# One-hots of both choices in one operation each, shared ports in the order model, and early stores on ScalarE

## The chip, the cores and the metric

The kernel runs on one core of a Trainium2 chip. A core has five engines that run beside each other, each through its own list of instructions in a fixed order: TensorE (PE, matrix products), VectorE (DVE), ScalarE (ACT), GpSimd (POOL) and SyncE (SP, which here only issues transfers). Data lies in DRAM and is brought by DMA queues into the on-chip memory SBUF; matrix products are written to PSUM. The metric is the time of one execution on the device in microseconds (us).

## The reference

Two stages. The first is a retention layer over q, k and v of shape [8 batches, 8 heads, 576 positions, 64]:

```
ret = (q k^T / 8) * D_h        D_h[i,j] = gamma_h^(i-j) for i >= j, else 0
x   = ret v                    -> 4608 tokens of 512 values
```

The second is a mixture of 8 experts. Each token gets noisy logits `x w_gate + log(1 + exp(x w_noise)) * noise`, and its two largest choose two experts, weighted by a softmax over the two. The output of a token is the sum over its two choices of

```
weight * ( relu(x w1[e]) w2[e] )      w1[e]: 512 x 1024,  w2[e]: 1024 x 512
```

## The kernel before

**Attention in units.** The 512 first positions are handled in 16 units, one for a batch and four of its heads. A unit loads q, k and v (`load`), scales and casts them to bf16 (`cast`: L436 for k, L442 for q, L449 for v), transposes them on PE (`tr`, L467), and then multiplies scores (`scores`, L492, masked on DVE at L500), carried states (`states`, L523) and outputs (`out_`, L555 and L565). The last 64 positions of a batch are the tails (`load_tail`, `tail`: L592, L601, L614, L619), two batches at a time.

**Routing per batch pair.** Two batches are a batch pair `bp`, 1152 tokens in 9 columns of 128. There are four, and each goes through `route` when its units and tails are done: logits, the two largest on DVE and POOL in some 25 small operations, the rank of each token within its expert by products with triangles of ones (L730, L732), and from the rank a place in the expert's list. The list itself, a table of the token number at each place, is built by a product of one-hots: `lof` and `hif` hold the low 7 bits of a place and the rest of it, for two choices x 9 columns. `olo` compares `lof` with 0..127 (L771), `oh` compares `hif` with 0..79 (L774), `oh` is multiplied by the token numbers `vals` (L777), and PE adds up the products of `olo` and `oh` over 18 pairs in a PSUM tile (`table`, L783), nine for each choice. DVE adds the result to the table so far and casts it to the list of rows `xi` (L790 to L796). Beside it, `route` puts the tokens with their payload (`pay`, L763 and L764, copied at L813) into rows that ACT stores to DRAM as `xd` (L816).

**Experts.** A tile is a group of rows of one expert. Rows are gathered from `xd` by `xi` with indirect transfers that POOL issues (`fetch`, L933), transposed on PE (L951), multiplied by w1 (`up`, L1005, or `wide`, L1031), passed through the relu (`relu`, L1014 on ACT or L1016 on DVE) and multiplied by w2 (`second`, L1080). `finish` scales the result by the gate. The first choice of a token goes to a DRAM buffer `yd` (evicted at L1114 or L1116, stored by SP at L1120), and the second one reads it back and adds it (L1095, L1124) and scatters the sum to the output (L1128). Tiles that the batch pairs 0 to 2 fill run early, for the experts 0 to 2, 15 blocks of 128 rows in all, between the units of the attention and behind the last route. The rest, which needs the last batch pair's list, runs afterwards as the wide phase, from 242 us of the profile on, where L1031 and L1080 alternate. Weights come through `weights`: those of experts 0 to 2 by casting transfers that POOL issues, the later ones by SP (L887 for w1, L890 for w2) into buffers of the class `big`, which the attention's inputs use before, and a cast by ACT or DVE.

**The order.** Nothing is issued where it stands in the code. `Plan.op` records an operation with its engine (or a choice of engines), an assumed cost, what it reads and writes, and a priority. `Plan.run` is a list scheduler: it keeps for each engine the time from which it is free, takes the ready operation that can start first, and appends it to the order. So each engine's fixed order comes from assumed costs, not measured times, and a change of one cost or engine can move operations everywhere. Transfers of SP and ACT share eight semaphores in turn; a transfer waits for the one that used its semaphore before. The lines of `run` that hold the model of time are

```
t = max(t0, free.get(e, 0.0))
...
free[e] = t + c
o.fin = t + c
```

In the profile `q` behind an engine's name is its issue of transfers, and PEld is PE's loading of the stationary operand.

Of the kernel before, what the change touches and what calls it, by code (L numbers as in the profile page):

```python
# [9 lines left out]
F16 = mybir.dt.float16  # L10
# [7 lines left out]
P = 128  # L18
# [32 lines left out]
class Op:  # L51
    __slots__ = ("i", "eng", "fn", "prio", "dma", "preds", "succ", "need", "allocs", "bufs", "fin", "on")


class Plan:
# [21 lines left out]
    def op(self, eng, cost, fn, r=(), w=(), prio=0.0, dma=0, after=()):  # L77
        o = Op()
        o.i, o.fn, o.prio, o.dma = len(self.ops), fn, prio, dma
        o.eng = eng if isinstance(eng, dict) else {eng: cost}  # L80
        o.succ, o.allocs, o.bufs = [], [], []
        preds = set(after)
        for items, wr in ((r, False), (w, True)):
            for it in items:
                b, sub = it if isinstance(it, tuple) else (it, None)
                for s2, o2, w2 in b.acc:
                    if (wr or w2) and (sub is None or s2 is None or s2 == sub):
                        preds.add(o2)
                if b not in o.bufs:
                    o.bufs.append(b)  # L90
        for items, wr in ((r, False), (w, True)):
            for it in items:
                b, sub = it if isinstance(it, tuple) else (it, None)
                if wr:
                    b.acc = [a for a in b.acc if a[1] is o or not (sub is None or a[0] == sub)]
                b.acc.append((sub, o, wr))
        preds.discard(o)
        for b in o.bufs:
            if b.cls is not None:
                if not b.ops:  # L100
                    o.allocs.append(b)
                    self.fifo.setdefault((b.cls, b.stream), []).append(b)
                b.ops.append(o)
                b.left += 1
        o.preds, o.need = preds, len(preds)
        for p in preds:
            p.succ.append(o)
        self.ops.append(o)
        return o

    def run(self):
        free, dma_free = {}, {}
# [33 lines left out]
        while ready:  # L146
            pick = None
            for o in ready:
# [38 lines left out]
            free[e] = t + c  # L187
            o.fin = t + c
# [39 lines left out]
class Kernel:  # L228
# [42 lines left out]
    def setup(self):  # L271
# [5 lines left out]
        def o(e, cost, b, fn, prio, r=()):  # L277
            pl.op(e, cost, lambda e: fn(), r=r, w=[b], prio=prio)
# [60 lines left out]
        vals = f("vals", [P, C9], F16)  # L339
        o("POOL", 0.2, vals, lambda: G.iota(vals.t, pattern=[[P, C9]], base=1, channel_multiplier=1, **n), 1)  # L340
# [79 lines left out]
    def cast(self, u):  # L420
# [16 lines left out]
        pl.op({"ACT": 1.06, "DVE": 0.7}, 0, k, r=[rk], w=[kn], prio=u)  # L437
# [5 lines left out]
        pl.op({"DVE": 1.23, "POOL": 1.91}, 0, q, r=[rq, tab], w=[qb], prio=u)  # L443
# [6 lines left out]
        for c in range(2):  # L450
            pl.op({"DVE": 0.69, "POOL": 1.06}, 0, lambda e, c=c: v(e, c), r=[(rv, c), tab], w=[(vn, c)], prio=u)
# [126 lines left out]
    def tail(self, bp, prio):  # L578
# [10 lines left out]
              else nc.vector.tensor_scalar_mul(qv(1), raw["k"].t, 0.125), r=[raw["k"]], w=[(qk, 1)], prio=prio)  # L589
        for j, n, o, b in ((8, "q", lambda: qv(0), (qk, 0)), (9, "v", vv, vt)):  # L590
# [3 lines left out]
                  r=[raw[n], tab], w=[b], prio=prio)  # L594
# [51 lines left out]
    def route(self, bp, prio):  # L646
# [7 lines left out]
        def o(e, cost, fn, r, w, prio=prio):  # L654
            return pl.op(e, cost, fn, r=r, w=w, prio=prio)
# [112 lines left out]
        iota, vals = self.fixed["iota"], self.fixed["vals"]  # L768
        olo, oh = f("olo", [P, 2, C, P], F16), f("oh", [P, 2, C, NH], F16)
        for j in range(2):  # L770
            o("DVE", 1.3, lambda e, j=j: V.tensor_tensor(  # L771
                olo.t[:, j], iota.t.unsqueeze(1).to_broadcast([P, C, P]), lof.t[:, j].unsqueeze(2).to_broadcast([P, C, P]),
                Alu.is_equal), [iota, lof], [(olo, j)])
            o("DVE", 0.9, lambda e, j=j: V.tensor_tensor(  # L774
                oh.t[:, j], iota.t[:, :NH].unsqueeze(1).to_broadcast([P, C, NH]),
                hif.t[:, j].unsqueeze(2).to_broadcast([P, C, NH]), Alu.is_equal), [iota, hif], [(oh, j)])
            o({"DVE": 0.9, "POOL": 1.4}, 0, lambda e, j=j: self.eng(e).tensor_tensor(  # L777
                oh.t[:, j], oh.t[:, j], vals.t.unsqueeze(2).to_broadcast([P, C, NH]), Alu.mult), [vals, (oh, j)], [(oh, j)])
        pT = self.psum("rt")

        def table(e, j):
            for c in range(C):
                nc.tensor.matmul(pT.t[:, :NH], lhsT=olo.t[:, j, c, :], rhs=oh.t[:, j, c, :],  # L783
                                 start=(j == 0 and c == 0), stop=(j == 1 and c == C - 1), skip_group_check=True)
        for j in range(2):
            o("PE", 0.6, lambda e, j=j: table(e, j), [(olo, j), (oh, j)], [pT])
# [313 lines left out]
    def finish(self, i, t, s, prio):  # L1100
# [8 lines left out]
        if k != "S":  # L1109
            y = pl.buf("half", "exp")  # L1110

            def ev(eng, y=y, po=po, g=g, n=n):
                if eng == "ACT":
                    nc.scalar.activation(y.t[:n], po.t[:n], Act.Copy, scale=g()[:n])  # L1114
                else:
# [4 lines left out]
            pl.op("SP", 0.07, lambda _, y=y, r0=r0, n=n: nc.sync.dma_start(out=self.yd[r0:r0 + n, :], in_=y.t[:n]),  # L1120
                  r=[y], w=[(key, j)], prio=prio, dma=0.7)
# [256 lines left out]
```

## Time and profile before

| what | value |
|---|---|
| time, median of 3 runs | 508.46 us (505.43 to 517.59) |
| time of the profiled execution | 505.94 us |
| span of the instructions in it | 504.4 us |
| PE busy | 419.5 us, 83% of the span |
| PE weight loads busy (beside PE) | 250.4 us, 50% |
| POOL busy | 303.2 us, 60% |
| ACT busy | 234.7 us, 47% |
| DVE busy | 199.8 us, 40% |
| mean granted TensorE clock | 0.927 of full speed |
| moved by DMA | 105.34 MB, mean 209 GB/s |

The span runs from the first to the last instruction; some 1.5 us of the execution lie around it. Times in the text are counted from the span's start. "L783" is line 783 of the kernel before. A wait is written as the instruction that waits, `<-`, and the instruction or transfer that ended last before it went on. Busy times are averages over parts of the kernel with different limits, so the text looks at windows of 20 us.

### The profile page before, as it was taken

What the parts mean: (1) busy time and instruction counts of PE and PEld (TensorE: products, weight loads), DVE (VectorE), ACT (ScalarE), POOL (GpSimd) and SP (SyncE); (2) the same over time, 40 slices, a digit from 0 to 9 for tenths busy, and PEclk for the clock granted to TensorE, in tenths of its full rate; (3) what the DMA queues carried; (4) which work ended last, traced back from release to release, by engine and by line L of the source; (5) the groups of instructions that cost most, each with busy time, mean ns of one, the idle gap of its engine ahead of it and who ended that gap; (6) DMA issues with size and microseconds to landing.
All of it is one profiled execution on the core that took longest, in us unless ns stands there. A gap on an engine that the chain in (4) does not pass through costs nothing. (4 is left out here: it accounts for less than half of the span.)

```text
span 504.4 us, 11045 instructions
## 1 busy us (share of the span) xinstructions
PE 419.5 (83%) x4253; PEld 250.4 (50%) x4288; DVE 199.8 (40%) x500; ACT 234.7 (47%) x397; POOL 303.2 (60%) x357
## 2 busy tenths in 40 slices
PE   1698948858678888729997999999899999899991
PEld 1476746646456667506544453453453453353450
DVE  3445697696348559500212333213214121121221
ACT  2476735556385556315654465545254242433330
POOL 8866599588769536773134544654756567357334
PEclk9995875888999989959998999999999999999997
DMA  7999979999698855434569797596589995525313
GB/s 188 304 248 305 241 218 302 226 287 209 171 187 141 206 94 179 144 98 128 216 205 339 239 329 244 161 313 239 167 265 371 254 214 180 153 103 189 109 52 138
DMA packets 102489, 105.34 MB, mean 209 GB/s; under 512 B 31870, under 2 KB 80511, under 8 KB 102434
## 3 DMA queue, kind: packets, MB, share of 16 engines
q1 hardware_dynamic: 82242, 62.85, 42.2%
q0 software_dynamic: 15264, 36.89, 28.1%
q10 hardware_dynamic: 4928, 4.87, 3.0%
q8 instruction: 34, 0.56, 0.5%
q14 instruction: 21, 0.17, 0.1%
HBM read 83.20 MB, written 26.63 MB: 218 GB/s over the span
## 5 line engine op out<-in xcount | busy, mean ns | idle before, releaser
L1080 PE MATMUL ps<-W,half 128*128 128x512 bf16 (+1 forms) x613 | 209.8, 391 | 22.0 <-issue 10.8
L1031 PE MATMUL ps<-big,W 128*128 128x512 bf16 (+4 forms) x632 | 187.2, 330 | 5.3 <-DVE half L1016 3.6
L1014 ACT ACTIVATE half<-ps 128x512 bf16<-128x512 f32 (+5 forms) x186 | 91.6, 505 | 155.1 <-PE ps L1031 85.4
L933 POOL DMA_INDIRECT xg<-xd,xi x80 | 83.1, 1039 | 80.3 <-ACT half L1114 29.7
L1080 PEld LDWEIGHTS <-half 128*128 128x128 bf16 (+1 forms) x640 | 63.1, 100 | 105.8 <-issue 38.3
L1031 PEld LDWEIGHTS <-W 128*128 128x128 bf16 x640 | 60.9, 98 | 56.5 <-issue 18.5
L1128 POOL DMA_INDIRECT out_dram<-half,xg x39 | 39.8, 1021 | 48.2 <-DVE half L1124 27.7
L1124 DVE SCALAR_TENSOR_TENSOR half<-ps,xg,half 128x512 f32<-128x512 f32 (+1 forms) x39 | 29.0, 749 | 88.8 <-PE ps L1080 52.2
L1095 POOL DMA_INDIRECT half<-yd,xg x39 | 39.6, 1016 | 11.9 <-issue 11.3
L262 ACT ACTIVATE half<-ps 128x1024 bf16<-128x1024 bf16 (+1 forms) x36 | 34.3, 988 | 17.0 <-DVE half L500 7.2
L500 DVE TENSOR_TENSOR half<-ps,mask 128x512 bf16<-128x512 f32 x64 | 40.0, 681 | 3.6 <-PE ps L492 2.6
L442 POOL TENSOR_TENSOR half<-big,tab 128x1024 bf16<-128x1024 f32 x15 | 29.5, 1967 | 12.6 <-DMA big<-in_q_dram 11.9
L467 PE MATMUL ps<-ident__69,half 128*128 128x128 bf16 x256 | 23.5, 259 | 11.7 <-ACT half L434 6.0
L449 POOL TENSOR_TENSOR half<-big,tab 128x512 bf16<-128x512 f32 x30 | 32.5, 1100 | 0.0
L1005 PE MATMUL ps<-half,W 128*128 128x256 bf16 (+1 forms) x288 | 30.5, 260 | 1.4 <-ACT tb L262 1.4
L523 PE MATMUL ps<-half,half 64*64 64x64 bf16 (+2 forms) x512 | 31.6, 235 | 0.2 <-issue 0.2
L1114 ACT ACTIVATE half<-ps,xg 128x512 f32<-128x512 f32 (+1 forms) x32 | 22.0, 688 | 16.8 <-PE ps L1080 9.8
L1005 PEld LDWEIGHTS <-W 128*128 128x128 bf16 x288 | 24.6, 100 | 6.0 <-issue 1.7
L262 ACT ACTIVATE xT<-ps 128x512 bf16<-128x512 f32 (+1 forms) x38 | 19.0, 554 | 15.6 <-PE ps L565 10.6
L467 PEld LDWEIGHTS <-half 128*128 128x128 bf16 x256 | 19.5, 118 | 13.2 <-ACT half L434 6.0
L523 PEld LDWEIGHTS <-half 128*64 128x64 bf16 (+1 forms) x512 | 19.5, 115 | 12.3 <-issue 4.1
L1124 DVE SCALAR_TENSOR_TENSOR half<-ps,gm,half 128x512 f32<-128x512 f32 x6 | 4.5, 751 | 52.8 <-ACT half L1114 35.0
(174 smaller groups left out, 455.7 us busy)
## 6 DMA issues: line engine op xcount, KB each, us to landing
big<-in_moe_w_dram SPq DMA_DIRECT2D x40, 512.0 KB
yd<-half SPq DMA_DIRECT2D x40, 256.0 KB
big<-in_k_dram SPq DMA_DIRECT2D x32, 256.0 KB
big<-in_q_dram SPq DMA_DIRECT2D x16, 512.0 KB
big<-in_v_dram SPq DMA_DIRECT2D x32, 256.0 KB
W<-in_moe_w_dram POOLq DMA_DIRECT2D x12, 512.0 KB
xd<-xg ACTq DMA_DIRECT2D x16, 264.0 KB
xg<-xd,xi POOLq DMA_INDIRECT x80
```

The costliest lines, as they stand in the source:

```text
L262: self.nc.scalar.activation(out, in_, Act.Copy)
L467: nc.tensor.transpose(v[:, hp, x, :], i[:, y, hp * P:(hp + 1) * P], ident.t)
L500: nc.vector.tensor_tensor(S.t.bitcast(BF16).rearrange("p (h c x) -> p h c x", h=2, c=2)[:, h], p[h].t.rearrange("p (c x) -> p c x", c=2), ...
L523: nc.tensor.matmul(o[h * HD:(h + 1) * HD, hp, n, :], lhsT=kv[0][:k, r, c, 2 * hp + h, :], rhs=m, start=(hp == 0 and c == 0 and k == P and ...
L933: pl.op("POOL", 1.3, lambda _, x=x, h=h, n=n: nc.gpsimd.indirect_dma_start(out=x.t[:n, :], out_offset=None, in_=self.xd[:rows, :], in_offs ...
L1005: nc.tensor.matmul(pv()[:, f2, :], lhsT=w.t[:, o:o + P], rhs=xv()[:, di, :n], start=(di == 0), stop=(di == KD - 1))
L1014: self.nc.scalar.activation(o, i, Act.Relu)
L1031: nc.tensor.matmul(p.t[:, :n], lhsT=w.t[:, o:o + P], rhs=xv()[:, di, :n], start=(di == 0), stop=(di == KD - 1))
L1080: self.nc.tensor.matmul(po.t[:n], lhsT=hv[:, s * P:s * P + n], rhs=self.W[e].t[:, o:o + DM], start=(f == 0), stop=(f == KF - 1))
L1095: pl.op("POOL", 1.3, lambda _, b=b, iy=iy, n=self.size(j): nc.gpsimd.indirect_dma_start(out=b.t[:n, :], out_offset=None, in_=self.yd[:rows ...
L1124: pl.op("DVE", 0.75, lambda _, o=o, b=b, po=po, g=g, n=n: nc.vector.scalar_tensor_tensor(o.t[:n], po.t[:n], g()[:n], b.t[:n], Alu.mult, Al ...
L1128: ins = nc.gpsimd.indirect_dma_start(out=self.out[:, :], out_offset=IOff(ap=io()[:n], axis=0), in_=o.t[:n, :], in_offset=None, bounds_chec ...
```

## The change

It has three parts.

1. **One-hots.** Both choices and all nine columns are made by one operation: `olo` becomes [128, 128, 18] and `oh` [128, 80, 18], with the 18 token columns innermost. For this, the counting operand is held with every number twice (`iota2`), and `lof` and `hif` are read in pairs. `oh` is multiplied by the token numbers in one operation, which now always runs on DVE. The table is one operation of 18 products, whose two operands are read with a step of 18 elements.
2. **Ports in the model.** An operation can be marked `port`. In `Plan.run`, a marked operation on DVE or POOL can't start before the last marked one on either of them has ended. Marked are the casts of the attention and the tails, and in `route` what runs on POOL or may run there, and DVE operations that read no PSUM tile. This changes no operation, only the order.
3. **Early stores.** The stores to `yd` of the early tiles (`t[2] < 3`, 15 of them) are issued by ACT, at an assumed cost of 0.3 us, and not by SP.

```diff
-    def op(self, eng, cost, fn, r=(), w=(), prio=0.0, dma=0, after=()):
+    def op(self, eng, cost, fn, r=(), w=(), prio=0.0, dma=0, after=(), port=False):
...
                 for e, c in o.eng.items():
                     t = max(t0, free.get(e, 0.0))
+                    if o.port and e in ("DVE", "POOL"):
+                        t = max(t, port[0])
...
             free[e] = t + c
+            if o.port and e in ("DVE", "POOL"):
+                port[0] = t + c
...
+        iota2 = f("iota2", [P, P, 2], F16)
+        o("POOL", 0.35, iota2, lambda: G.iota(iota2.t, pattern=[[1, P], [0, 2]], base=0, channel_multiplier=0, **n), 1)
...
-        pl.op({"DVE": 1.23, "POOL": 1.91}, 0, q, r=[rq, tab], w=[qb], prio=u)
+        pl.op({"DVE": 1.23, "POOL": 1.91}, 0, q, r=[rq, tab], w=[qb], prio=u, port=True)
...
         def o(e, cost, fn, r, w, prio=prio):
-            return pl.op(e, cost, fn, r=r, w=w, prio=prio)
+            port = e == "POOL" or isinstance(e, dict) or e == "DVE" and not any(
+                (b[0] if isinstance(b, tuple) else b).cls == "ps" for b in r)
+            return pl.op(e, cost, fn, r=r, w=w, prio=prio, port=port)
...
-        olo, oh = f("olo", [P, 2, C, P], F16), f("oh", [P, 2, C, NH], F16)
-        for j in range(2):
-            o("DVE", 1.3, lambda e, j=j: V.tensor_tensor(
-                olo.t[:, j], iota.t.unsqueeze(1).to_broadcast([P, C, P]), lof.t[:, j].unsqueeze(2).to_broadcast([P, C, P]),
-                Alu.is_equal), [iota, lof], [(olo, j)])
-            o("DVE", 0.9, lambda e, j=j: V.tensor_tensor(
-                oh.t[:, j], iota.t[:, :NH].unsqueeze(1).to_broadcast([P, C, NH]),
-                hif.t[:, j].unsqueeze(2).to_broadcast([P, C, NH]), Alu.is_equal), [iota, hif], [(oh, j)])
-            o({"DVE": 0.9, "POOL": 1.4}, 0, lambda e, j=j: self.eng(e).tensor_tensor(
-                oh.t[:, j], oh.t[:, j], vals.t.unsqueeze(2).to_broadcast([P, C, NH]), Alu.mult), [vals, (oh, j)], [(oh, j)])
+        olo, oh = f("olo", [P, P, 2 * C], F16), f("oh", [P, NH, 2 * C], F16)
+        pairs = lambda a, n: a.rearrange("p j c -> p (j c)").rearrange("p (a x) -> p a x", x=2).unsqueeze(1).to_broadcast([P, n, C, 2])
+        for dst, src, n, c in ((olo, lof, P, 1.36), (oh, hif, NH, 0.92)):
+            o("DVE", c, lambda e, dst=dst, src=src, n=n: V.tensor_tensor(
+                dst.t.rearrange("p n (a x) -> p n a x", x=2), iota.t[:, :n].unsqueeze(2).to_broadcast([P, n, C, 2]),
+                pairs(src.t, n), Alu.is_equal), [iota, src], [dst])
+        o("DVE", 0.92, lambda e: V.tensor_tensor(
+            oh.t, oh.t, vals.t.unsqueeze(1).to_broadcast([P, NH, 2 * C]), Alu.mult), [vals, oh], [oh])
...
-                nc.tensor.matmul(pT.t[:, :NH], lhsT=olo.t[:, j, c, :], rhs=oh.t[:, j, c, :],
-                                 start=(j == 0 and c == 0), stop=(j == 1 and c == C - 1), skip_group_check=True)
...
+                nc.tensor.matmul(pT.t[:, :NH], lhsT=olo.t[:, :, c], rhs=oh.t[:, :, c],
+                                 start=(c == 0), stop=(c == 2 * C - 1), skip_group_check=True)
+        o("PE", 1.2, table, [olo, oh], [pT])
...
-            pl.op("SP", 0.07, lambda _, y=y, r0=r0, n=n: nc.sync.dma_start(out=self.yd[r0:r0 + n, :], in_=y.t[:n]),
-                  r=[y], w=[(key, j)], prio=prio, dma=0.7)
+            pl.op(*(("ACT", 0.3) if t[2] < 3 else ("SP", 0.07)), lambda q, y=y, r0=r0, n=n: self.eng(q).dma_start(
+                out=self.yd[r0:r0 + n, :], in_=y.t[:n]), r=[y], w=[(key, j)], prio=prio, dma=0.7)
```

In the order that results, against the order before: PE's order in the wide phase is unchanged, and ahead of it the table products of the routes 0 and 1 stand further forward among the attention's work. On DVE, casts and masks that stood inside route 0's chain (L436, L449, two of L500) follow the one-hots; on POOL the larger casts (L442, L449, L592) follow the routes' operations, and L777 is gone. On ACT each of the 15 stores follows its eviction L1114. On SP the first four weight transfers of expert 3 (L887) stand directly behind the tail loads of the last batch pair, with no store ahead of them. In route 3 the payload (L763) follows the operations of `overflow_list`'s `cT`.

More of the change, by code (lines that the diff above doesn't have):

```diff
@@ L436, in k @@
                 nc.vector.tensor_scalar_mul(o, i, 0.125)
[L437 removed]
+        pl.op({"ACT": 1.06, "DVE": 0.7}, 0, k, r=[rk], w=[kn], prio=u, port=True)
         def q(e):
@@ L779, in route @@
-        pT = self.psum("rt")
-        def table(e, j):
-            for c in range(C):
-                nc.tensor.matmul(pT.t[:, :NH], lhsT=olo.t[:, j, c, :], rhs=oh.t[:, j, c, :],
-                                 start=(j == 0 and c == 0), stop=(j == 1 and c == C - 1), skip_group_check=True)
-        for j in range(2):
-            o("PE", 0.6, lambda e, j=j: table(e, j), [(olo, j), (oh, j)], [pT])
+        iota, vals = self.fixed["iota2"], self.fixed["vals"]
+        olo, oh = f("olo", [P, P, 2 * C], F16), f("oh", [P, NH, 2 * C], F16)
@@ L787, in route, with table @@
+        pT = self.psum("rt")
+        def table(e):
+            for c in range(2 * C):
+                nc.tensor.matmul(pT.t[:, :NH], lhsT=olo.t[:, :, c], rhs=oh.t[:, :, c],
+                                 start=(c == 0), stop=(c == 2 * C - 1), skip_group_check=True)
+        o("PE", 1.2, table, [olo, oh], [pT])
         L = f("L", [P, NH])
```

17 lines of the change are left out of this document (8 added, 9 removed).

## The prediction

> **What bounds the kernel now.** I read the page first for the engines' shares. PE is busy for 83% of the span, and no other engine passes 60%. The chain that ended last is of no use here: it holds only the register work behind the last scatter. So I read PE's idle time, first by stretches and then by its releasers. Two gaps stand in the first half, at 60 to 80 and 100 to 120 us, and a third one at 200 to 242. From 280 to 480 PE works 193.5 of 200 us. In the next lines the columns are window, its length, and each engine's busy time with the number of its instructions; the granted clock and the DMA share stand behind.
>
> ```profile
> 60.00:80.00 20.00, 10.86 (x249) 9.10 (x246) 18.67 (x40) 9.80 (x16) 17.41 (x26) 0.72 0.79 219
> 100.00:120.00 20.00, 13.52 (x293) 10.90 (x290) 18.70 (x43) 9.86 (x16) 17.67 (x27) 0.83 1.02 268
> 140.00:160.00 20.00, 15.99 (x265) 11.86 (x267) 14.37 (x39) 13.62 (x22) 15.26 (x26) 0.99 0.86 156
> 200.00:220.00 20.00, 11.98 (x90) 7.49 (x91) 8.22 (x24) 6.47 (x13) 15.06 (x14) 0.89 0.44 130
> ```
>
> In the first two windows DVE (third busy figure) and POOL (fifth) are full while PE is not. The list of waits (total, times, longest), and then PE's timeline (start, duration, idle before and its releaser) name the place:
>
> ```profile
> PE ps L783 <- POOL oh L777: 12.6, 3, 6.0
> ```
>
> ```profile
> 77.16 0.76 PE L783 MATMUL ps<-oh,olo 128*128 128x80 f16 x9 [5.22 <-POOL oh L777]
> ...
> 112.44 0.76 PE L783 MATMUL ps<-oh,olo 128*128 128x80 f16 x9 [5.99 <-POOL oh L777]
> ...
> 160.48 0.48 PE L783 MATMUL ps<-oh,olo 128*128 128x80 f16 x9 [1.44 <-POOL oh L777]
> ```
>
> PE runs a fixed order, and three of the four table products (L783) stand in it before their operand is ready: 12.6 us. The fourth, at 195.58, waits 0.77 for L832, another operation. PE's order is the bound up to 242 us; an idle stretch removed there moves everything behind it.
>
> **One-hots, removed and added.** The groups give the removed operations:
>
> ```profile
> L771 DVE TENSOR_TENSOR olo<-iota__66,lof x8: 1345/1360/2205, 70.4 to 192.0; 128x1152 f16<-128x1152 f16 x8
> ...
> L774 DVE TENSOR_TENSOR oh<-iota__66,hif x8: 894/896/2087, 71.7 to 193.2; 128x720 f16<-128x720 f16 x8
> ...
> L777 POOL TENSOR_TENSOR oh<-oh,vals x8: 1378/1382/2576, 75.7 to 195.8; 128x720 f16<-128x720 f16 x8
> ```
>
> A route spends 2 x (1.36 + 0.90) = 4.5 us on DVE and 2 x 1.38 = 2.8 on POOL. The new three DVE operations hold 2304, 1440 and 1440 elements. No row shows this shape. At the old rate they take 2 x 1.36 + 2 x 0.90 + 2 x 0.90 = 6.3 us. At the rate of the nearest faster row (L264, a copy of 1024 bf16 from PSUM, 0.69 us, 0.67 ns an element) they take 1.55 + 0.97 + 0.97 = 3.5. I take 3.5, because the old operand lof repeats one value along the innermost run, as L264's never does, and in the new form two neighbouring elements stand innermost in every operand; 6.3 stays as a bound. The Trainium skill, VectorE: DVE Perf Modes, section "What auto-detection actually checks", says that a two-tensor operation runs at two elements a cycle if every tensor is 16-bit with step one; whether a run of only two elements counts, no run here shows.
>
> Two-tensor operations of DVE and POOL also hold each other up. At 72.55 an L771 took 2.21 instead of 1.36 beside POOL's copies L813 (73.49, 2.28), and at 111.06 an L774 took 2.09 instead of 0.90 beside L777 (109.81, 2.58). The new order keeps such pairs apart as far as its model's times hold; I count only what moves out of the chains.
>
> *Route 0.* hif was written at 70.28. L436 (0.70) and L449 (0.82), which stood in this chain, now follow it: 1.5 us earlier. Then 3.5 us on DVE end at 68.9 + 3.5 = 72.4; the table started at 77.16, so 4.8 earlier. But in the new order the table stands ahead of inter, xtr, tltr and tlsc, which filled part of the old wait (0.94 + 0.51 + 0.62 + 0.32 = 2.4), and behind one more batch of states (1.1): 1.3 us of that work is still to do. **-3.5.** At 6.3 us: -0.7.
>
> *Route 1.* L755 took 1.84 instead of 0.17 beside POOL's cast L442, which moves out of the chain: 1.7 earlier, so 105.1 + 3.5 = 108.6. PE had nothing from 106.45 on; now 16 UP products (8 in 1.04 to 1.34) fill 2.1 us or more, up to 108.6. The whole 5.99 may go; **-5.0**, as those products need a finished transpose of gathered rows. At 6.3 us: about -3.1.
>
> *Route 2.* 154.6 + 3.5 = 158.1, and PE is busy until 159.04: **-1.4**. At 6.3 us: 0.
>
> *Route 3.* No wait on the one-hots, nothing gained. Its payload copy L763 now follows 15 small operations (196.04 to 199.87 before), so bp3's rows are stored about 3 us later and gathered later. From its last rank (186.7) PE had 55 us of early work left before the wide phase (242.2), and the new order leaves some 6 us more: 0. If that cover is gone, 3.
>
> **Table operands.** The 18 products of a route now read both operands with a step of 18 elements (36 bytes). Nine took 0.48 us at full clock, 53 ns a pair. The nearest row, L732, reads rows in runs of 8 elements and takes 0.49 for nine: nothing extra. A quarter of the speed as the far end costs 72 x 160 ns = 11.5 us over four routes. I take half the speed at half the places, **+2.0**. The Trainium skill, SBUF — State Buffer, in its note on "cachelines", speaks against this change: neighbours that do not share a 16-byte line pay a penalty. Its size it does not give, and the trace before has no matmul with such a step.
>
> **Stores.** The 15 stores of early tiles leave SP for ACT, right behind their evictions (L1114). ACT's own stores L816 cost 0.366 us at the median, up to 1.204: 15 x 0.37 = 5.5 us on the engine that also runs the relus (L1014) PE waits for. ACT is 47% busy, so about half meets waiting work: **+3.0**; bounds 0 and 5.5. ACT's lane waits in front of L816 were at most 38 ns. SP loses its in-order blocks: one store waited 25.4 us for L1114, and the tail loads of the last batch pair, queued behind, went at 140 to 149 us; the first weights of expert 3 went at 238.5. Both now go earlier. In the wide phase one wait may go with it, 3.60 us at 272.88, which ended at a gather that landed while the next weights loaded (DMA share 0.88 in 260 to 280): half of it, **-1.8**; bounds 0 and -3.6.
>
> **Clock.** PE was granted 0.72 and 0.83 in the two windows with waits, and less where it had been full before (0.62 in 40 to 60). Fuller windows may cost as much as they save: 0, bounds -3 and +3.
>
> **Sum.** Against the profiled execution (505.94; span 504.4 and 1.5 around it): 505.9 - 3.5 - 5.0 - 1.4 - 1.8 + 2.0 + 3.0 = **499.2**. That execution lies 2.5 below the median of 508.46, at the low end of 505.43 to 517.59, so 499 is 1.3% under the one and 1.8% under the other. About 2% is what a measurement of this kernel can tell from no change.
>
> **Rivals.**
> - *The stride slows the table*, the slower side. 72 pairs on PE, 53 ns each now. My gains without the term are 8.7 us, so from 53 + 121 = 174 ns a pair on, the change loses. At 213 ns: 499.2 - 2.0 + 11.5 = 508.7. For it: a step no row shows. Against: L732. Chance 0.12.
> - *The one-hots stay at the old rate.* -3.8 instead of -9.9: 505.3. For it: every two-input f16 row of DVE shows 1.2 ns an element. Chance 0.12. Both together, 514.8: 0.06.
> - *The stall at 211 to 229 changes.* PE stood 4.33, 3.97 and 4.71 us there, put to "issue" and to L1014, while POOL issued 19 gathers in a row (200.98 to 226.7) and SP its stores. I do not know its cause. Other gathers and stores in that place could remove 8 of the 13 us (491; 0.14) or add one gap of 5 (504; 0.06).
> - *ACT's stores hold up relus.* If each costs the longest L816, 1.2 us, with nothing hidden, 18 us take the place of 3: 514. It decides from 0.78 us each on (11.7, which is 3.0 and the gain together is gone). Chance 0.08.
> - The forecast, 495 to 503, keeps 0.42.
>
> **From these cases:** faster by over 2% of the median (under 498.3) is half of the forecast and the 491 case, 0.35. Slower by over 2% are the two cases near 514 where a second cost (the clock's +3, say) comes on top, 0.14. The rest, 0.51, lies within 2%. The range goes from 488 (the 491 case with the wide wait gone) to 514.
>
> **What the changed profile would show.** Right: olo near 1.4 to 1.6 us and the two others near 0.9 to 1.0; no PE wait on POOL before the table, and at most 3 us on DVE at route 0; nine table products in about 0.5 us at full clock; ACT stores of about 0.4 us each; the wait near 273 shorter. Wrong: olo at 2.7; table pairs over 170 ns; relus that wait behind a store for its lane; a larger gap between 200 and 242; or PE idle moved to later places of its order, where transposes and casts that were moved out of the chains come too late.

## The result and the profile after

The changed kernel is slower by 1.1%: the ratio of its times to those of the kernel before, run side by side, is 1.0109, with a 95% interval of 1.0068 to 1.0149. The interval leaves out no change and lies on the other side of it than the forecast (499.2 us, 1.3 to 1.8% faster), inside the 2% that count as the same. The median of its 20 executions is 510.41 us (506.17 to 520.43), that of 20 of the kernel before 511.75 us (503.48 to 521.32). The ratio leaves out executions more than 1.5% above the fastest of the same kernel, and the kernel before had the lower fastest one, so the two plain medians stand the other way round. The profiled execution took 506.17 us (before 505.94) with a span of 504.6 (504.4) at a mean granted clock of 0.925 (0.927): by the profiles, no change.

What was to become faster did. The groups of the changed kernel (line, engine, operation, durations in ns as minimum, median and maximum, first and last start) for the one-hots, the multiplication and the table:

```profile
L780 DVE TENSOR_TENSOR olo<-iota,lof x4: 1351/1352/1353, 66.7 to 178.5; 128x2304 f16<-128x2304 f16 x4
L780 DVE TENSOR_TENSOR oh<-iota,hif x4: 901/902/904, 68.0 to 179.8; 128x1440 f16<-128x1440 f16 x4
...
L783 DVE TENSOR_TENSOR oh<-oh,vals x4: 908/911/919, 68.9 to 180.7; 128x1440 f16<-128x1440 f16 x4
...
L789 PEld LDWEIGHTS <-olo x72: 139/142/146, 68.1 to 186.5; 128*128 128x128 f16 x72
L789 PE MATMUL ps<-oh,olo x72: 306/328/332, 69.9 to 186.6; 128*128 128x80 f16 x72
```

Twice the elements take the time of the old operation, 0.59 ns an element where it was 1.18. But every product of the table became longer, 328 ns at the median where it was 214 in the kernel before:

```profile
L783 PE MATMUL ps<-oh,olo x72: 196/214/275, 77.2 to 197.5; 128*128 128x80 f16 x72
```

PE's timeline (start, duration, idle before and its releaser) shows the tables and the largest new wait:

```profile
69.91 2.82 PE L789 MATMUL ps<-oh,olo 128*128 128x80 f16 x18 [3.03 <-DVE oh L783]
...
103.45 1.37 PE L561 MATMUL ps<-half,half 64*64 64x128 bf16 x32 [4.99 <-DVE nl L683]
...
118.37 2.83 PE L789 MATMUL ps<-oh,olo 128*128 128x80 f16 x18
...
184.14 2.83 PE L789 MATMUL ps<-oh,olo 128*128 128x80 f16 x18
...
275.07 0.32 PE L1036 MATMUL ps<-big,W 128*128 128x192 bf16 x1 [3.82 <-DVE im L980]
```

The waits on POOL ahead of the tables, 12.6 us, are gone, 3.03 us on DVE are left, and a wait of 4.99 us stands where there was none. The wait in the wide phase is as long as it was (3.60 us at 272.88 before). The windows that showed PE idle in the kernel before read like this now (window, length, busy time of PE, weight loads, DVE, ACT, POOL; granted clock, DMA share):

```profile
60.00:80.00 20.00, 13.25 (x216) 10.70 (x217) 13.79 (x40) 8.70 (x13) 16.09 (x27) 0.67 0.85 242
...
100.00:120.00 20.00, 13.43 (x160) 10.64 (x161) 9.95 (x36) 10.93 (x18) 12.49 (x23) 0.57 1.05 269
...
140.00:160.00 20.00, 17.57 (x430) 13.38 (x429) 14.30 (x44) 14.76 (x26) 13.81 (x27) 1.00 1.03 262
...
200.00:220.00 20.00, 9.57 (x60) 4.48 (x58) 0.00 (x0) 2.35 (x4) 14.85 (x15) 0.75 0.43 122
```

From 60 to 80 PE works 2.4 us more; from 100 to 120 no more than before; and between 200 and 220 it works 9.57 of 20 us (11.98 before). The wide phase begins at 244.2 us (242.2). The next two lines are the whole stretch ahead of it, the first of the kernel before, the second of the changed one:

```profile
0.00:242.20 242.20, 177.77 (x2967) 132.95 (x2977) 135.49 (x391) 125.88 (x198) 168.99 (x225) 0.87 0.82 205
```

```profile
0.00:244.20 244.20, 187.17 (x2966) 140.63 (x2978) 119.81 (x385) 124.97 (x196) 154.33 (x221) 0.86 0.81 209
```

PE's idle time fell from 242.2 - 177.8 = 64.4 to 244.2 - 187.2 = 57.0 us, a gain of 7.4. Its busy time for the same products grew by 9.4. So the question for the experiments is where 9.4 us of busy time come from, and why the gain in idle time is not larger.

### The profile page after: what moved, and what is told of

Its sections match the earlier page's. It is cut to its first block, busy times and chain, and to the rows that moved or that the text cites. A ratio compares the mean times of both kernels' runs of the same rounds, so it can differ in the third digit from the quotient of the medians.

```text
span 504.6 us, 11041 instructions
## 1 busy us (share of the span) xinstructions
PE 428.4 (85%) x4252; PEld 258.1 (51%) x4288; DVE 183.9 (36%) x494; ACT 233.4 (46%) x396; POOL 288.1 (57%) x353
## 5 line engine op out<-in xcount | busy, mean ns | idle before, releaser
L1085 PE MATMUL ps<-W,half 128*128 128x512 bf16 (+1 forms) x612 | 208.0, 388 | 11.4 <-ACT half L1019 5.5
L1019 ACT ACTIVATE half<-ps 128x512 bf16<-128x512 f32 (+5 forms) x185 | 90.1, 503 | 157.8 <-PE ps L1036 94.6
L938 POOL DMA_INDIRECT xg<-xd,xi x80 | 84.6, 1057 | 81.4 <-ACT half L1119 35.4
L1085 PEld LDWEIGHTS <-half 128*128 128x128 bf16 (+1 forms) x640 | 62.7, 100 | 95.3 <-issue 27.1
L1036 PEld LDWEIGHTS <-W 128*128 128x128 bf16 x640 | 61.0, 98 | 53.4 <-issue 15.0
L1010 PE MATMUL ps<-half,W 128*128 128x256 bf16 (+1 forms) x288 | 33.5, 270 | 6.8 <-issue 4.9
L1119 ACT ACTIVATE half<-ps,xg 128x512 f32<-128x512 f32 (+1 forms) x34 | 23.4, 687 | 25.0 <-PE ps L1085 14.4
L266 ACT ACTIVATE half<-ps 128x1024 bf16<-128x1024 bf16 (+1 forms) x31 | 29.9, 997 | 10.6 <-PE ps L607 7.6
L448 POOL TENSOR_TENSOR half<-big,tab 128x1024 bf16<-128x1024 f32 x14 | 26.8, 1911 | 12.6 <-DMA big<-in_q_dram 7.7
L1010 PEld LDWEIGHTS <-W 128*128 128x128 bf16 x288 | 25.9, 103 | 14.2 <-issue 9.3
L498 PE MATMUL ps<-half,half 64*64 64x128 bf16 x512 | 13.2, 248 | 13.1 <-ACT half L266 9.8
```

Source lines behind the costliest of these rows:

```text
L938: pl.op("POOL", 1.3, lambda _, x=x, h=h, n=n: nc.gpsimd.indirect_dma_start(out=x.t[:n, :], out_offset=None, in_=self.xd[:rows, :], in_offs ...
L1010: nc.tensor.matmul(pv()[:, f2, :], lhsT=w.t[:, o:o + P], rhs=xv()[:, di, :n], start=(di == 0), stop=(di == KD - 1))
L1019: self.nc.scalar.activation(o, i, Act.Relu)
L1036: nc.tensor.matmul(p.t[:, :n], lhsT=w.t[:, o:o + P], rhs=xv()[:, di, :n], start=(di == 0), stop=(di == KD - 1))
L1085: self.nc.tensor.matmul(po.t[:n], lhsT=hv[:, s * P:s * P + n], rhs=self.W[e].t[:, o:o + DM], start=(f == 0), stop=(f == KF - 1))
```

## The experiments

The kernels ran in five groups, each on one chip beside the kernel before. On three of the chips the kernel before had medians of 512, 508 and 508 us; on the other two (runs e5 to e8, and e17 and e18) 473 and 474. Ratios are always to the kernel before on the same chip. Each edit below is to the changed kernel unless it says otherwise.

**The table's step.** To take away the step alone, the low and high parts and the token numbers are written twice side by side, so that the counting index can lie innermost in `olo` and `oh` and both operands of DVE still have two neighbours. Every engine has the order of the changed kernel.

```diff
-lof, hif = ... f("lof", [P, 2, C], F16), f("hif", [P, 2, C], F16)
+lof, hif = ... f("lof", [P, 2 * C, 2], F16), f("hif", [P, 2 * C, 2], F16)     # every value twice
-olo, oh = f("olo", [P, P, 2 * C], F16), f("oh", [P, NH, 2 * C], F16)
+olo, oh = f("olo", [P, 2 * C, P], F16), f("oh", [P, 2 * C, NH], F16)
-lhsT=olo.t[:, :, c], rhs=oh.t[:, :, c]
+lhsT=olo.t[:, c, :], rhs=oh.t[:, c, :]
```

> The changed kernel with one thing else: lof, hif and vals are written twice side by side, and the one-hots lie with the counting index innermost, so the table's operands are read without a step. Every engine's order is that of the changed kernel. Theory: the step costs PE 157 - 53 = 104 ns a pair, 72 pairs, 7.5 us, all in PE's fixed order. Then nine pairs take about 0.5 us again, and the kernel takes 5 to 7.5 us less than the changed one (ratio to the kernel before about 0.995 to 1.000 if the changed one stands at 1.01). Rival: PE's order is not the bound in these stretches, and the gain goes into idle time in front of later work, above all the stall at 204 to 222 us; then less than 2 us less than the changed one.

Measured: 0.9961 (0.9912 to 1.0009), median 509.71 us. The one-hots take the same 1.35 and 0.90 us, and the table's products are short again:

```profile
L791 PEld LDWEIGHTS <-olo x72: 97/100/143, 71.3 to 189.8; 128*128 128x128 f16 x72
L791 PE MATMUL ps<-oh,olo x72: 199/202/268, 73.0 to 189.9; 128*128 128x80 f16 x72
```

So the step, and not the 16-bit type or the number of products, makes them long. What it costs in time was measured twice with equal orders on one chip. First without ports and with stores on SP (the one-hots alone, with the step and without):

```diff
 # the change's one-hots on the kernel before; no port=, stores on SP
-oh.t, oh.t, vals.t.unsqueeze(2)...      (two operations a choice, POOL multiplies)
+the changed kernel's three operations   (e5: with the step; e6: without it, as in the diff above)
```

> The kernel before with one part of the change alone: the one-hots of both choices in one operation, token columns innermost; no shared ports in the model, stores on SP. Theory: the route's waits on POOL go (12.6 us in the profile), DVE's three operations end 3 to 5 us earlier, and the table costs 7.5 us more: ratio to the kernel before 0.995 to 1.005. Rival: the port model, not the one-hots, is what costs, and this kernel is 1% faster than the kernel before.

Measured: 1.0081 (1.0049 to 1.0112), median 476.87 us.

> The same with the counting index innermost and each low and high part written twice side by side, so that the table's operands have no step; every engine's order is that of the run with the strided one-hots alone. Theory: 5 to 7.5 us faster than that one, ratio to the kernel before 0.983 to 0.995. Rival: what PE gains stands as idle time in the crawl between 200 and 230 us, and the two are the same within 2 us.

Measured: 1.0011 (0.9978 to 1.0044), median 473.85 us. The step costs 476.87 - 473.85 = 3.0 us there. The other pair is the changed kernel itself (e15) and the run without the step again (e16), on a third chip:

> The changed kernel itself, beside the run with the pause and the one without the step. Theory: 1.0 to 1.5% slower than the kernel before on a chip that crawls, and 0.8 to 1.5% on one that does not. Rival: the same within 0.5% on a chip that does not crawl.

> The changed kernel with the counting index innermost in the one-hots, so that PE reads the table's operands without a step; the other engines' orders are those of the changed kernel. Theory: 3 us (0.6%) or more faster than the changed kernel on the same chip, as in the two runs without ports. Rival: the same within 0.3%; then PE's order is not what bounds the changed kernel.

Measured: 1.0130 (1.0027 to 1.0233), median 507.69 us (the kernel before: 507.69 too), and 1.0031 (0.9911 to 1.0150), median 504.08: 3.6 us. The intervals of this pair overlap; with the first pair, whose intervals do not, the step stands at 3 to 4 us of the 6.3 that the profile shows on PE. So part of the step's time reaches the end; for the orders without ports that is shown, for those of the changed kernel it rests on two medians. But the one-hots, even without the step, gain nothing measurable by themselves (1.0011). The trace of that run (e6) shows waits on DVE at two of the tables, where the kernel before waited for POOL:

```profile
75.58 1.36 PE L791 MATMUL ps<-oh,olo 128*128 128x80 f16 x18 [2.40 <-DVE oh L785]
...
114.31 1.17 PE L791 MATMUL ps<-oh,olo 128*128 128x80 f16 x18 [3.17 <-DVE half L506]
```

That is 5.6 of the 12.6 us. Where the other 7.0 are lost is not shown: no trace of the kernel before was taken on this chip.

**The port order.**

```diff
-return pl.op(e, cost, fn, r=r, w=w, prio=prio, port=port)
+return pl.op(e, cost, fn, r=r, w=w, prio=prio)          # and no port=True on the casts
```

> The changed kernel without the shared ports in the order model: casts and the routes' operations of DVE and POOL may be planned beside each other again. Theory: the port order brought the last rank from 186.7 to 175.5 us in the profile; without it 3 to 6 us of this are lost, and the kernel gets 2 to 5 us slower than the changed one. Rival: the pairs that hold each other up are off PE's path, and the two are the same within 2 us.

Measured: 0.9983 (0.9937 to 1.0029), median 509.87 us, on the chip of e1. It had been expected 2 to 5 us slower than the changed kernel, and nothing of that is seen; the changed kernel itself did not run on this chip. The wait at 103 us is not in its trace. The changed kernel's list of waits names where that wait begins, and ACT's timeline gives the place:

```profile
ACT half L594 <- DMA half<-in_k_dram: 9.8, 1, 9.8
```

```profile
101.75 0.63 ACT L594 ACTIVATE half<-half 128x512 bf16<-128x512 f32 x1 [9.77 <-DMA half<-in_k_dram]
102.29 0.21 ACT L680 ACTIVATE nl<-ps 128x72 f32<-128x72 f32 x1
```

```profile
102.83 0.23 DVE L682 TENSOR_TENSOR nl<-nl,noise 128x72 f32<-128x72 f32 x1 [7.11 <-ACT nl L681]
103.16 0.23 DVE L683 TENSOR_TENSOR nl<-nl,ps 128x72 f32<-128x72 f32 x1
```

With the ports in the model, the cast of the tails' k (L594) was planned on ACT ahead of the exponential of the second route's logits (L680). In the model its data was there. On the chip the load had not landed, ACT stood for 9.77 us, the logits' chain stood behind it, and PE stood 4.99 us for the PSUM tile that L683 releases. In the kernel before, the same cast (L588 there) came behind that operation (L672 there) and waited for nothing:

```profile
97.18 0.23 ACT L672 ACTIVATE nl<-ps 128x72 f32<-128x72 f32 x1 [2.33 <-PE ps L666]
...
106.96 0.63 ACT L588 ACTIVATE half<-half 128x512 bf16<-128x512 f32 x1
```

The 5.99 us that PE lost at the table of this route are gone, but a new wait of 4.99 us stands 15 us ahead of that table. The same wait of 6 to 11 us on ACT is in the traces of all runs that have ports and the new one-hots (11.2 in e1, 6.2 in e8), and not in e4 and e6, which have no ports. What it costs at the end of the kernel no run shows by itself.

The ports alone, on the kernel before:

```diff
 # before.py with port= in op(), run() and on the casts; one-hots and stores as before
```

> The kernel before with the shared ports in the order model alone; old one-hots, stores on SP. Theory: the port order moves the wait of the second route ahead of the rank instead of removing it, and the last stretch holds more work: 0.5 to 1.5% slower than the kernel before. Rival: without contention DVE's and POOL's operations get shorter and the kernel is 0.5 to 1% faster.

Measured: 1.0037 (0.9991 to 1.0083), median 504.56 us. No difference is shown: the interval takes in no change, and the plain median is the lowest of its group (the kernel before: 507.64). In this order the cast waited 0.4 us for its load; so it is the order that ports and one-hots give together that has the long wait, not the ports as such.

**The stores.**

```diff
-pl.op(*(("ACT", 0.3) if t[2] < 3 else ("SP", 0.07)), ...
+pl.op(*("SP", 0.07), ...
```

> The changed kernel with the early stores back on SP. Theory: 15 x 0.33 us = 5 us of issue on ACT lie mostly beside idle time of ACT, 0 to 2 us on the path; SP's blocks come back (tail loads of the last batch pair behind a store, weights of expert 3 behind 14 stores), which costs 0 to 4 us: within 2 us of the changed kernel, either way. Rival, as predicted: half of the 5 us was on the path, and the kernel gets 2 to 5 us faster than the changed one.

Measured: 1.0054 (0.9985 to 1.0124), median 509.08 us. And the stores alone on the kernel before (the same line the other way):

> The kernel before with the early stores on ACT alone. Theory: 15 x 0.33 us lie beside idle time of ACT, and SP's earlier loads bring nothing that PE waits for: within 0.5% of the kernel before. Rival, as predicted: 3 us slower (0.6%) by held-up relus.

Measured: 1.0083 (1.0013 to 1.0154), median 508.24 against 507.64. Both point to a cost of the stores on ACT of 0.1 to 0.8%, and neither is sharp enough to tell 0 from 4 us. On the chip of e1, e3 and e4 the three medians lie within 0.8 us (509.71, 509.08, 509.87), whichever part was taken away. In the profile the 15 issues cost 0.326 us each, 4.9 us in all, and each waited 17 ns for its lane, so the case of relus held up behind a lane is out.

The changed kernel once more, and the kernel before with the one-hots without a step and the stores on ACT (no ports), on the chip of e10 and e11:

> The changed kernel itself, to stand on one chip beside its parts. Theory: the step of the table's operands (7.5 us of PE, of which 3 us showed in the pair of runs with one order) and the port order's new waits (L561 at 103 us, 4.99 us, which the kernel before did not have; L498 at 23 us, 3.6 instead of 1.4) cost more than the waits at the tables gave back: 1.0 to 2.0% slower than the kernel before. Rival: the loss is the crawl at 200 to 225 us and its size from execution to execution; on a chip that does not show the crawl the two are the same within 0.5%.

> The kernel before with the one-hots made in one operation with the counting index innermost (no step for PE), and the early stores on ACT; no ports in the model. Theory: the best of the parts: 0 to 1% faster than the kernel before. Rival: the one-hots' gain of 12.6 us of waits is hidden by later waits (2.4 us at the first table, 3.2 at the second, for DVE), and it is the same within 0.5%.

Measured: 1.0118 (1.0045 to 1.0190) and 1.0129 (1.0073 to 1.0184). By the ratio the changed kernel repeats its loss; its plain median is 508.69 us, against 507.64. The second (median 508.94) was expected to be the best of the parts and is not: on this chip nothing that the one-hots save shows at the end. It is e4 without the step, and e4 stood at 0.9983 on its chip. By that the step would make a kernel 1.5% faster, where e5 and e6 show it to cost 3.0 us. So ratios from two chips that crawl can differ by more than the parts are worth, and setting one against the other tells nothing about a part. The profile of e12 shows the wide phase from 247.7 us on, although its last rank came at 184.7. That led to the stretch between the two.

**The crawl between the last rank and the wide phase.** In the changed kernel PE is idle for 15.1 of the 68.7 us between its last rank (175.5) and the wide phase, in the kernel before for 14.6 of 55.5 (ends less starts of the products in the trace). While POOL issues 18 gathers one behind the other, a gather every 1.3 us, PE stops again and again with nothing in the profile to wait for ("issue"), here in the changed kernel:

```profile
207.60 0.27 PE L1010 MATMUL ps<-half,W 128*128 128x128 bf16 x2 [1.09 <-issue]
...
209.73 0.22 PE L956 MATMUL ps<-ident__69,xg 128*128 128x128 bf16 x1 [1.80 <-issue]
...
215.15 1.03 PE L1085 MATMUL ps<-W,half 128*128 128x512 bf16 x2 [3.01 <-issue]
```

This is called the crawl here. To take the unbroken run away, POOL fills a dead tile with zeros behind each gather; the other engines keep their orders.

```diff
 pl.op("POOL", 1.3, <gather>, ...)
+if early == 3 and self.nspc < 20:
+    self.nspc += 1
+    pl.op("POOL", 0.01, lambda _: nc.gpsimd.memset(<olo, all 2304 elements>, 0.0), ..., after=[pl.ops[-1]])
```

> The changed kernel with one thing else: behind each of the first 20 gathers of the last lists POOL fills a dead tile with zeros, so gathers no longer follow each other without a pause. PE's, DVE's, ACT's and SP's orders are those of the changed kernel. Theory: the crawl of PE between 204 and 222 us (one or a few products every 0.7 us, 12 us idle) comes from the unbroken run of 18 gathers, 196 to 219 us: with pauses PE's idle time there falls below 4 us and the kernel gets 6 to 10 us faster than the changed one, as long as the last gather still lands before 240 us. Rival: PE's own supply of instructions is late there, or it waits for ACT; then the crawl stays, 10 to 13 us, and the time is the same or longer.

Measured: 1.0089 (1.0042 to 1.0136), median 517.76 us. The crawl is gone: PE works 19.89 of the 20 us from 200 to 220 (9.57 in the changed kernel), and the wide phase begins at 235.4, on a chip on which e1, e3 and e4 crawl. But the pause was 2.03 us long, so a gather went only every 3.2 us. The wide phase then waited 12.1 us in one place for the late rows, and the whole gain was lost. Two shorter pauses, 576 and 1152 elements instead of 2304:

> The changed kernel with a pause behind each of the first 20 gathers of the last lists, a quarter of the one before: 576 elements, about 0.5 us, so a gather every 1.7 us and not every 1.3. Theory, with the crawl shown to come from the unbroken run and the loss of the long pause from late gathers: the last of the 18 gathers goes at about 228 us, in time for the wide phase; if a gather every 1.7 us is slow enough, the crawl goes and the kernel gets 6 to 9 us faster than the changed one. Rival: what counts is how many gathers are under way, and at 1.7 us they still pile up; then the crawl stays and the time is the same.

> The same with 1152 elements, about 1.0 us, a gather every 2.2 us. Theory: no crawl; the last of the 18 gathers goes at about 237 us, just as the wide phase begins to need them: 3 to 9 us faster than the changed kernel. Rival: the wide phase waits for gathers as with the long pause (two waits, 4.3 and 12.1 us), and most of the 9 us is given back.

Measured: 1.0172 (1.0132 to 1.0212) and 1.0249 (1.0213 to 1.0284), medians 481.51 and 485.13. These two runs came on a chip that doesn't crawl. There e5 and e6, whose gathers follow each other without a pause, have this window of PE (e5):

```profile
200.00:220.00 20.00, 19.84 (x164) 13.55 (x166) 2.10 (x10) 12.03 (x20) 15.43 (x16) 1.00 0.68 208
```

So the run of gathers is not enough by itself; the chip has a part in it, and what that is no trace here shows. On this chip the expectation of e7 could not be tested, and e7 shows something else: the changed kernel with a pause loses 1.7% without any crawl. A pause of this length costs the one-hots without a step next to nothing on another chip of about that time (e17 below, 1.0002, beside e6, 1.0011), so most of the 1.7% is, by this argument, the change's own price: 0.7% is the step (1.0081 against 1.0011), and the rest stands with the ports' order and the stores. The traces fit it. These are the first products of the wide phase in e5 and in e7, 6.5 us apart:

```profile
218.26 6.39 PE L1036 MATMUL ps<-big,W 128*128 128x448 bf16 x33
```

```profile
224.76 6.38 PE L1040 MATMUL ps<-big,W 128*128 128x448 bf16 x33
```

What follows takes 255 us in both, and from 200 to 220 PE works 19.84 us in both. So e7 is late ahead of the gathers, and not by rows that come late.

The same pause came on a chip that crawls with the last group but one, on both kernels:

```diff
-memset(<olo, all 2304 elements>, 0.0)
+memset(<olo, 576 elements>, 0.0)            # e13: on the kernel before; e14: on the changed one
```

> The kernel before with the short pause (576 elements, 0.5 us) behind each of its first 20 gathers of the last lists; all other engines' orders are its own. Theory: on a chip where PE crawls during the unbroken run of gathers, the crawl (14.6 us idle and a lowered clock behind it, between the last rank and the wide phase) goes or shrinks, and the kernel gets 1 to 3% faster than the kernel before; on a chip without the crawl it gets 0 to 1% slower, by gathers that come later. Rival: a gather every 1.7 us still piles up, and PE crawls as before: the same within 0.5%.

> The changed kernel with the same short pause. Theory: as for the kernel before, 1 to 3% faster than the changed kernel on a chip that crawls. Without the crawl the wide phase begins near 225 us, and what is left against the kernel before with its pause is the price of the change itself: 0.5 to 1.5% slower than that one. Rival: the crawl is the cause of the whole loss, and the two with a pause are the same within 0.5%.

Measured: 0.9689 (0.9504 to 0.9873), median 493.91 us, and 0.9770 (0.9659 to 0.9882), median 490.91 us, against 507.69 for each kernel without a pause. The windows of the changed kernel without (e15, first) and with the pause (e14), same chip, same orders of PE, DVE, ACT and SP:

```profile
200.00:220.00 20.00, 12.77 (x92) 7.47 (x90) 1.72 (x7) 4.80 (x8) 14.96 (x16) 0.80 0.46 128
220.00:245.00 25.00, 21.24 (x147) 12.83 (x147) 2.43 (x11) 9.98 (x19) 7.95 (x8) 0.82 0.32 99
```

```profile
200.00:220.00 20.00, 20.00 (x158) 13.71 (x157) 3.42 (x13) 9.95 (x18) 17.21 (x21) 1.00 0.45 134
220.00:245.00 25.00, 25.00 (x180) 14.74 (x179) 5.22 (x13) 14.31 (x28) 22.11 (x27) 1.00 0.45 128
```

And POOL's timeline of the same two, at the start of the run:

```profile
203.16 1.00 POOL L938 DMA_INDIRECT xg<-xd,xi  x1 [0.30 <-issue]
204.47 0.95 POOL L938 DMA_INDIRECT xg<-xd,xi  x1 [0.31 <-issue]
205.72 1.01 POOL L938 DMA_INDIRECT xg<-xd,xi  x1 [0.30 <-issue]
```

```profile
204.55 0.96 POOL L939 DMA_INDIRECT xg<-xd,xi  x1 [0.30 <-issue]
205.51 0.59 POOL L944 MEMSET olo<- 128x576 f16 x1
206.27 1.02 POOL L939 DMA_INDIRECT xg<-xd,xi  x1 [0.17 <-issue]
```

A gather every 1.75 us instead of every 1.3 takes the crawl away, and with it the lowered clock behind it (0.80 and 0.82 become 1.00). The wide phase begins at 230.4 us instead of 246.8, and the kernel takes 16.8 us less. That the unbroken run brings the crawl about is shown on two chips (e2, e14) by taking away only this run; that the kernel gets faster by it, on one. Which of the two kernels is better with the pause these runs do not settle: the ratios favour the kernel before, the medians the changed one.

**The best of it.** The kernel before, with the one-hots without a step, no ports, stores on SP, and a pause, of 576 and of 288 elements:

> The kernel before with the one-hots in one operation, the counting index innermost (no step for PE), and the short pause of 576 elements; no ports in the model, stores on SP. Theory: what the one-hots gain at the tables (waits of 12.6 us less 5.6 that stay) shows only once the crawl is out of the way: at least as fast as the kernel before with the pause (ratio 0.96 to 0.975 on a chip that crawls), and the best of all. Rival: PE is held by DVE and by loads there, and it stands at the 0.97 of the kernel before with the pause, or above.

> The same with a pause of half the length, 288 elements, about 0.3 us: a gather every 1.5 us. Theory: if the gap between gathers is what matters, the crawl stays away, and the earlier gathers spare some of the wait of 3.7 to 4.7 us that the wide phase has near 253 to 261 us: 0 to 3 us faster than with 576. Rival: at 1.5 us the gathers pile up and PE crawls, in part or fully: 5 to 15 us slower than with 576.

Measured, on a chip where the kernel before takes 474 us, as on the one that doesn't crawl (no kernel without a pause was profiled on it): 1.0002 (0.9968 to 1.0037) and 0.9945 (0.9917 to 0.9974), medians 475.06 and 471.86 against 474.05. The second is the only kernel that beats the kernel before on either of these two chips, by half a percent. What a pause of 288 elements does on a chip that crawls was not run, so how short the gap may be stays open.

## Why the prediction was wrong, point by point

- **What bounds the kernel:** right in the place of the waits, wrong in what they were worth, and this is the failed step that weighs most: "an idle stretch removed there moves everything behind it". The three waits were to bring 9.9 us, 3.2 of them by casts that move out of the chains. The one-hots alone, without the step, brought nothing (1.0011 in e6): 5.6 us of the waits are still there, on DVE, and what the rest turned into stays open.
- **One-hots, 3.5 us on DVE:** right, 1.35 + 0.90 + 0.91 = 3.16 us. The rule that I quoted (the Trainium skill, VectorE: DVE Perf Modes, "What auto-detection actually checks") holds here for runs of two elements: 0.59 ns an element. The rival of the old rate is out.
- **Route 0, -3.5:** the mechanism was right. The table began at 69.9 us (72.4 forecast), behind a rank that came 2.5 us sooner, and the wait fell from 5.22 to 3.03. But the table took 2.82 us instead of 0.76 + 0.78, which eats 1.3 of it.
- **Route 1, -5.0:** wrong, and the clearest failure in a single term. I took the chain's start from the old order less the one contention I saw (L755), 105.1 us. In the changed order the chain began late: its rank came at 106.7 instead of 101.8 and hif at 110.44 instead of 106.67, because ACT stood behind a tail load. I had looked at what the order moves on PE, DVE and POOL around the chain, not at what it puts in front of the chain on ACT. The table of this route began at 118.4 us, 6 us later than before.
- **Route 2, -1.4:** the wait on POOL went, and its table took 1.9 us more than before.
- **Table operands, +2.0:** the mis-sized term, and the next failure. Eighteen products take 2.83 us, 157 ns a pair instead of 53, at the full clock and at half of it alike (2.83 us at 184.14, with 1.00 granted; 2.82 us at 69.91, with 0.56): 7.5 us over four routes against the full clock's 53 ns, and against the actual 0.76 + 0.81 and 0.48 + 0.48 of the old tables 1.3 + 1.3 + 1.9 + 1.9 = 6.3 us. My bound of 213 ns was not far off; I took less than a fifth of its 11.5 us because L732 reads runs of eight without loss, and a run of one element is not near a run of eight. The rule that speaks against the change (the Trainium skill, SBUF — State Buffer, the note on "cachelines") told the sign: at 36 bytes each element has a line of its own, and the pair takes three times as long. By the rival's own point of decision, 174 ns, the step alone would still have left a small gain; with route 1 gone it did not.
- **Stores, +3.0:** not refuted. 0.326 us each instead of 0.366; between 0 and 4 us in all. SP's earlier loads brought nothing that can be seen: weights of expert 3 went from 141 us on and not from 238.5, but the wait in the wide phase, for which I had counted -1.8, is still there (3.82 us).
- **Route 3 and the rest of the order:** the last rank came 11.2 us sooner, and the wide phase 2.0 later. That was no loss to a new wait: the new order leaves 32 products of L1010, about a dozen of L1085 and 8 transposes more behind the rank, and one table of 2.83 us, and the crawl is as long as before (15.1 us against 14.6).
- **The crawl, a rival at 0.14 and 0.06:** it did not change with the change. Its cause, which I had left unknown, is the unbroken run of gathers, on some chips.
- **The range:** its lower end, 488, should have been 489.4 by its own terms, 499.2 - 8.0 - 1.8.

Summed over the stretch ahead of the wide phase, idle time fell by 7.4 us, near what the terms for the waits gave together, and busy time grew by 9.4: 6.3 of it is the table, and 3.1 are other products, which fits a lower granted clock (0.86 against 0.87 in the mean, 0.57 in the window of the new wait): 192 products of one form (L1010, L1005 before) took 296 ns in the mean instead of 280. The clock's term, put at 0 with bounds of 3, came out at its bound. This sum is worked out from one execution of each, and it gives 2 us, not 1.1%.

What was measured at the end of the kernel is 3 to 4 us for the step, and on the chip that doesn't crawl 4.6 us more for the ports' order, the stores and a pause together (481.51 in e7, 476.87 in e5), not told apart. That the gain of 1.3 to 1.8% is not there, every run of the changed kernel says. How large the loss is stays open: the ratio gave 1.1 to 1.3% three times, the plain medians -0.3, +0.2 and 0.0%.

## What to carry to other kernels

Where an engine waits in a fixed order, ask for every new order which operation now stands in front of the chain on each engine, also on those that the change does not name: here a cast that waited for a load moved ahead of the logits, and PE stood 4.99 us where 5.99 were to be gained. A layout that gives one engine two elements at a time can cost another one three times its reading time; where both read the same tile, write the small operand twice rather than turn the large one. And measure on more than one chip before a stall is put down to the program alone: a pause of 0.6 us behind each gather was worth 3% on a chip that crawls, and nothing on one where the kernel is 7% faster to begin with.

## What the runs showed of the hardware

- 16-bit operations of two tensors on DVE took 0.59 ns an element when pairs of neighbours stood innermost in all operands, even where the pair is repeated with a step of zero around it, and 1.18 ns when one operand repeated a single value.
- A TensorE product whose two 16-bit operands have a step of 36 bytes took 157 ns for 128 stationary and 80 moving columns, at full and at half granted clock alike, and 53 ns without the step at the full clock.
- On three chips PE stood still again and again while POOL issued an unbroken run of indirect gathers, one every 1.3 us, from 5 to 10 us after the run's begin to a few us behind its end. Between the last rank and the wide phase PE was idle for 12 to 19 us in the traces of these chips without a pause. With a gather every 1.75 us this did not appear on one of them (2.7 us idle in e14), and on a fourth chip it did not appear with one every 1.3 us either (0.3 us in e5 and e6). What differs between the chips stays open.
